# Cosformer attention ahead of a mixture of experts: the reciprocal denominators of batches 3 to 7 reach the features by DMA through DRAM

## The chip, the cores and the metric

The kernel runs on one core of a Trainium2 chip. The metric is device time in microseconds (us), lower is better; the median of six runs of the kernel before is 1002.9 us (1001.9 to 1004.23).

## The reference

Two stages follow each other. In the first, for each of 8 batches and 8 heads (576 positions s, 64 channels d), a linear attention is computed:

```python
q_p, k_p = concat([relu(x) * cos_w, relu(x) * sin_w])   # 128 features f
kv  = einsum('bhsf,bhsd->bhfd', k_p, v)
z   = k_p.sum(over s)
num = einsum('bhsf,bhfd->bhsd', q_p, kv)
den = einsum('bhsf,bhf->bhs', q_p, z) + 1e-6
attn = num / den                                        # one den for the 64 channels of a head
```

Its result, 4608 tokens x 512 channels, is the x of the second stage. There the 8 gate columns exp(x @ w_gate) are normalized over rows and columns eight times (Sinkhorn), and the output is the sum over 8 experts e of P[:, e] * (relu(x @ w1[e]) @ w2[e]), with w1[e] of 512 x 1024 and w2[e] of 1024 x 512.

## The kernel before, in words

x is held transposed in SBUF as `xT` (128 partitions hold two heads' 64 channels each; four such parts `hk` make up the 512 channels). The first phase interleaves two things in blocks j = 0 to 6, each of 16 slots: expert 0 on the token block j (512 tokens), and the attention of batch b = j + 1 (576 tokens). Slots 0 to 7 hold one `ffn1` step each (four matmuls of 512 columns, then a relu on ScalarE into `hT`); slots 8 to 15 hold half an `ffn2` each (four matmuls of 512 columns), and every second one ends with a copy of `y_ps` into the accumulator `acc`, on ScalarE for even tiles g and on VectorE for odd ones. After its matmuls a slot runs what the table `todo` lists for it, filled by `at(block, slot, fn, ...)`. Since `te`, `ve` and `se` pin the written order on TensorE, VectorE and ScalarE, the order in which these functions are called is the order of each engine's queue. POOL (GpSimd) and SP (SyncE) issue DMAs; their queues are in written order too.

The functions of the attention are, per batch:

- `load` (POOL): q, k and v of two of the four `hk`, six DMAs a batch, float32 in DRAM to float16 in SBUF, four buffers each (two batches).
- `prep_k` (relu of k, ScalarE), `prep_q` (q times cos and sin, VectorE), `prep_kv` (k times cos and sin, and v copied beside a column for z, both VectorE).
- `turn` (12 a batch): three 128-column matmuls transpose a third of a q_p into one bank of the pool `ps_s` (named small_ps, four banks), and ScalarE or VectorE, in turns, moves it with a relu to `q_pT`.
- `sums` (2 a batch): k_p times v into two banks of `ps_s`; VectorE writes `zsel`, then ScalarE `kv_sb`.
- `denominators`: 24 matmuls give den for 8 heads on 96 partitions (3 parts j of 32 rows, of which 8 differ); VectorE adds 1e-6 / 64 and takes the reciprocal, then splits it into the float16 pair `hi` and `hl`.
- `attend` (4 a batch, one for each hk): three matmuls with 0/1 weights (`spread`) bring the reciprocals of two heads to their 128 channel partitions in two banks, ScalarE copies them to `rb` in SBUF, four matmuls give the numerators in two more banks, and VectorE multiplies the two into `xT`.
- `gates`: the logits of a batch and their exp.

In block j from 1 on, `denominators` of batch j + 1 is in slot 5 and its attends are in slots 8, 10, 12 and 14, with the gates of batch j in slot 6. `ffn1` of block j + 1 reads the `xT` of batch j + 1. The last two thirds of the `turn`s of a batch, two in each of the slots 0 to 4, are in the same block as its attends; the preparation of the next batch (`ahead`) is in slots 6 to 15, its first two turns in slot 15.

After block 6 the second phase takes over the SBUF and PSUM of the first: token blocks 7 and 8 of expert 0, the Sinkhorn steps, then experts 1 to 7. `x_sums` there saves sums of `xT` to DRAM (`x_saved`) on SP's queue.

Of the kernel before, what the change touches and what calls it, by code (L numbers as in the profile page):

```python
# [25 lines left out]
def kernel(  # L26
# [10 lines left out]
    nc = tc.nc  # L37
# [44 lines left out]
    def not_before(earlier, i):  # L82

        if earlier is not None:
# [4 lines left out]
                reason="written order",  # L89
            )  # L90

    class InOrder:

        def __init__(self, engine):
# [51 lines left out]
    def ffn2(hT, w, c0, g, y_ps, fts):  # L146

        for ft in fts:
            te.matmul(
                out=y_ps,  # L150
                lhsT=hT[:, ft, c0 : c0 + P],
                rhs=w[1][:, ft, :],
                start=(ft == 0),
                stop=(ft == FT - 1),
            )
        if FT - 1 in fts:

            if g % 2 == 0:
                se.copy(out=acc(g), in_=y_ps)
            else:  # L160
                ve.tensor_copy(out=acc(g), in_=y_ps)
# [10 lines left out]
    with ExitStack() as p1:  # L172
# [4 lines left out]
        qp_pool = p1.enter_context(tc.tile_pool(name="qp_pool", bufs=3))  # L177
        qT_pool = p1.enter_context(tc.tile_pool(name="qT_pool", bufs=6))
        kv_pool = p1.enter_context(tc.tile_pool(name="kv_pool", bufs=2))
        rb_pool = p1.enter_context(tc.tile_pool(name="rb_pool", bufs=2))  # L180
        ps_y = p1.enter_context(tc.tile_pool(name="ps_y", bufs=2, space=bass.MemoryType.PSUM))
        ps_s = p1.enter_context(tc.tile_pool(name="ps_s", bufs=4, space=bass.MemoryType.PSUM))

# [1 line left out]
        loaded = {}  # L185
        sources = {"q": q, "k": k, "v": v}

        def load(b, half, names="qkv"):
            for name in names:
                x = ld.tile([P, 2, C, D], F16, name=f"{name}_ld")  # L190
                view = sources[name][b].rearrange("(hk hh) (p c) d -> (hh p) hk (c d)", hh=2, c=C)
                nc.gpsimd.dma_start(
                    out=x[:].rearrange("p hk c d -> p hk (c d)"),
                    in_=view[:, 2 * half : 2 * half + 2],
                )
                for i in range(2):
                    loaded[name, b, 2 * half + i] = x[:, i]

# [88 lines left out]
        ve.tensor_copy(out=wg[:], in_=wg_ld[:])  # L287


        kps, qps, qTs, kvs, hls = {}, {}, {}, {}, {}  # L290
        v_augs = [cs_pool.tile([P, C, D + 2], F16, name=f"v_aug{i}") for i in range(4)]
        for t in v_augs:
            ve.memset(t[:, :, D : D + 1], 1.0 / XS)

# [82 lines left out]
        def denominators(b):  # L377

            zsel = kvs[b][1]
            den_ps = ps_s.tile([P, 512], FP32, name="small_ps")  # L380
            for h in range(H):
                hk, hh = h // 2, h % 2
                for j in range(3):
                    te.matmul(
                        out=den_ps[32 * j : 32 * j + 32, 0 : C3 * HP],
                        lhsT=zsel[:, h, :],
                        rhs=qTs[b, hk][:, j * C3 : (j + 1) * C3, hh * HP : (hh + 1) * HP],
                        start=(h == 0),
                        stop=(h == H - 1),
                    )  # L390
            den = kv_pool.tile([96, C3 * HP], FP32, name="den")
            ve.tensor_scalar(
                out=den[:], in0=den_ps[0:96, 0 : C3 * HP], scalar1=1e-6 / XS, scalar2=None,
                op0=ALU.add,
            )
            ve.reciprocal(out=den[:], in_=den[:])

            hi = kv_pool.tile([96, C3 * HP], F16, name="hi")
            ve.tensor_copy(out=hi[:], in_=den[:])
            hl = kv_pool.tile([96, C3 * HP], F16, name="hl")  # L400
            ve.scalar_tensor_tensor(
                out=hl[:], in0=hi[:], scalar=lo[0:96], in1=den[:], op0=ALU.mult, op1=ALU.add
            )
            hls[b] = hl

        def attend(b, hk):

            parts = ((0, 2 * C3), (2 * C3, C))
            rb_ps = [ps_s.tile([P, 512], FP32, name="small_ps") for _ in parts]
            rb = rb_pool.tile([P, C * HP], FP32, name="rb")  # L410
            for i, (c0, c1) in enumerate(parts):
                for j in range(c0 // C3, c1 // C3):
                    te.matmul(
                        out=rb_ps[i][:, (j * C3 - c0) * HP : ((j + 1) * C3 - c0) * HP],
                        lhsT=spread[0:96, j, hk].rearrange("p hh d -> p (hh d)"),
                        rhs=hls[b][:],
                        start=True,
                        stop=True,
                    )
                se.copy(out=rb[:, c0 * HP : c1 * HP], in_=rb_ps[i][:, 0 : (c1 - c0) * HP])  # L420
            num_ps = [ps_s.tile([P, 512], FP32, name="small_ps") for _ in parts]
            for i, (c0, c1) in enumerate(parts):
                for hh in range(2):
                    te.matmul(
                        out=num_ps[i][hh * HP : (hh + 1) * HP, 0 : (c1 - c0) * HP],
                        lhsT=kvs[b][0][:, hk, hh, :],
                        rhs=qTs[b, hk][:, c0:c1, hh * HP : (hh + 1) * HP],
                        start=True,
                        stop=True,
                    )  # L430
                ve.tensor_tensor(
                    out=xT[:, hk, b * S + c0 * HP : b * S + c1 * HP],
                    in0=num_ps[i][:, 0 : (c1 - c0) * HP],
                    in1=rb[:, c0 * HP : c1 * HP],
                    op=ALU.mult,
                )
# [89 lines left out]
        for j in range(B):  # L526
            b = j + 1
            if j == 0:

                at(0, 4, lambda: begun.append(sums_begun(1, 0)))  # L530
                at(0, 5, lambda: sums_made(1, 0, begun[2]))
                at(0, 6, lambda: begun.append(sums_begun(1, 1)))
                at(0, 7, prep_q, 1, 0)
                at(0, 7, prep_q, 1, 1)
                for hk in range(HK):
                    for i in range(3):
                        at(0, 7 + hk, turn, 1, hk, i)
                    if hk == 0:
                        at(0, 7, lambda: sums_made(1, 1, begun[3]))
                    if hk < 2:  # L540
                        at(0, 7 + hk, prep_q, 1, hk + 2)
                at(0, 10, denominators, 1)
                at(0, 11, gates, 0)
                for hk in range(HK):
                    at(0, min(13 + hk, 15), attend, 1, hk)
            elif b < B:
                at(j, 0, prep_q, b, 3)
                at(j, 1, prep_kv, b, 3)
                at(j, 1, sums, b, 0)
                at(j, 3, sums, b, 1)  # L550
                for i, (hk, k_) in enumerate(turns[2:]):
                    at(j, i // 2, turn, b, hk, k_)
                at(j, 5, denominators, b)
                for hk in range(HK):
                    at(j, FT + 2 * hk, attend, b, hk)
            if j:
                at(j, 6, gates, j)
            if b + 1 < B:
                for half in range(2):
                    at(j, 2 * half if j else 3, load, b + 1, half)  # L560
                for i, (fn, hk) in enumerate(ahead):
                    at(j, NS - 10 + i if j else 11 + i // 2, fn, b + 1, hk)
                for hk, k_ in turns[:2]:
                    at(j, NS - 1, turn, b + 1, hk, k_)
        y_pss = {}
        for j in range(B - 1):
            if j:
# [172 lines left out]
    class Pair:  # L740
# [23 lines left out]
                op0=ALU.mult, op1=ALU.add,  # L764
            )

        def sums(self, after=None):
            name = "hs_last" if self.last else "hs"
            pool = u_pool if self.last else hs_pool
            S1, S2, S4 = (pool.tile([P, FH, P], F16, name=f"{name}{k_}") for k_ in (1, 2, 4))  # L770
            for out_, in0, in1, op in (
                (S1[:], self.a21, self.a22, ALU.add),
                (self.a21, self.a11, self.a21, ALU.subtract),
                (S2[:], S1[:], self.a11, ALU.subtract),
                (S4[:], self.a12, S2[:], ALU.subtract),
            ):
                i = (nc.gpsimd if self.last else ve).tensor_tensor(  # L777
                    out=out_, in0=in0, in1=in1, op=op
                )
                if self.last and after is not None:  # L780
                    tc.add_manual_dep(
                        i.ins,
                        after.ins.name,
                        mybir.DependencyInfo(
                            mybir.DependencyClass.Sync, mybir.DependencyReason.DATA
                        ),
                        reason="VectorE's sums first",
                    )
                    after = None
            self.summed = i  # L790
            self.S1, self.S2, self.S4 = S1[:], S2[:], S4[:]

# [303 lines left out]
```

The softmax here doesn't subtract the row's maximum and nothing guards it: scores larger than these inputs give would overflow.

## Time and profile before

| | |
|---|---|
| Median of six runs | 1002.9 us |
| The profiled execution's own time | 1002.74 us |
| Its span in the trace | 1001.0 us |
| TensorE busy | 983.0 us (98%) |
| VectorE, ScalarE, POOL busy | 829.4, 575.3, 60.3 us |
| Blocks 1 to 5, each | 22.2 us |
| Block 6 | 22.0 us |

PE is TensorE's matmuls, PEld its weight loads, DVE is VectorE, ACT ScalarE, SPq the DMA queue of SP. Matmuls overlap in the array, so their listed durations add up to more than the time they hold the engine; the differences between their starts are what a matmul costs its queue. A bracket at the end of a timeline line tells how long the engine sat idle before that instruction and what ended the wait. Helper objects record every engine's operations, so that nearly all instructions of the first phase have line L100; tiles (out<-in) tell them apart. TensorE's start times in one block (the one from 96.59 us, j = 3) are used below as prices.

### The profile page before, as it was taken

What the parts mean: (1) busy time and instruction counts of PE and PEld (TensorE: products, weight loads), DVE (VectorE), ACT (ScalarE), POOL (GpSimd) and SP (SyncE); (2) the same over time, 40 slices, a digit from 0 to 9 for tenths busy, and PEclk for the clock granted to TensorE, in tenths of its full rate; (3) what the DMA queues carried; (4) which work ended last, traced back from release to release, by engine and by line L of the source; (5) the groups of instructions that cost most, each with busy time, mean ns of one, the idle gap of its engine ahead of it and who ended that gap; (6) DMA issues with size and microseconds to landing.
All of it is one profiled execution on the core that took longest, in us unless ns stands there. A gap on an engine that the chain in (4) does not pass through costs nothing.

```text
span 1001.0 us, 20629 instructions
## 1 busy us (share of the span) xinstructions
PE 983.0 (98%) x8062; PEld 691.2 (69%) x8062; DVE 829.4 (83%) x1862; ACT 575.3 (57%) x1284; POOL 60.3 (6%) x82
## 2 busy tenths in 40 slices
PE   8999999999999999999999999999999999999997
PEld 7555555446777777777777777777777777777775
DVE  5888777588989887888879878888889888988887
ACT  5766666447777555555555555555555555555552
POOL 6321200001000000000000000000000000000001
PEclk8999999999999999999999999999999999999999
DMA  9956510533101331034013320043113410104535
GB/s 172 199 86 93 82 28 1 99 75 74 41 25 49 66 67 48 26 71 86 25 40 71 57 62 26 24 91 66 33 40 67 83 32 25 48 25 105 136 85 127
DMA packets 51922, 66.50 MB, mean 66 GB/s; under 512 B 4848, under 2 KB 43760, under 8 KB 51824
## 3 DMA queue, kind: packets, MB, share of 16 engines
q0 software_dynamic: 27232, 30.94, 19.9%
q1 hardware_dynamic: 24352, 33.98, 12.3%
q8 instruction: 63, 1.03, 0.4%
q14 instruction: 35, 0.29, 0.1%
q10 hardware_dynamic: 240, 0.26, 0.1%
HBM read 83.12 MB, written 12.98 MB: 96 GB/s over the span
## 4 chain that ended last, share of the span: by engine, by line
PE 72%; issue 21%; DVE 5%; ACT 1%; POOL 1%; DMA 1%; POOLq 0%; ACTq 0%; DVEq 0%
PE rows_ps L100 25%; PE h_ps L100 21%; PE copied_ps L100 8%; PE p_ps L100 8%; PE y_ps L100 5%; PE small_ps L100 5%; DVE k_p L100 1%; DMA k_ld<-in_k_dram 1%; DVE q_pT L100 1%; DVE v_aug L100 0%; DVE q_p L100 0%; DVE den L100 0%; DVE xT L100 0%; DVE acc_lo L100 0%; POOL hs_last L777 0%
## 5 line engine op out<-in xcount | busy, mean ns | idle before, releaser
L762 DVE SCALAR_TENSOR_TENSOR acc_lo<-rows_ps,P_tok,acc_lo 128x512 f32<-128x512 f32 (+1 forms) x322 | 203.1, 639 | 74.8 <-PE rows_ps L100 74.6
L100 PEld LDWEIGHTS <-H 128*128 128x128 f16 x2080 | 203.0, 98 | 83.1 <-issue 1.2
L698 ACT CAST u<-h_ps 128x384 f16<-128x384 f32 x288 | 137.8, 478 | 131.1 <-PE h_ps L100 131.1
L100 PEld LDWEIGHTS <-w1e 128*128 128x128 f16 x1632 | 155.8, 98 | 59.3 <-issue 4.9
L692 DVE CUSTOM_DVE_ANT_0 H<-p_ps,u 128x384 f16<-128x384 f32 x329 | 180.9, 550 | 6.7 <-PE p_ps L100 6.6
L100 PEld LDWEIGHTS <-hs 128*128 128x128 f16 x1500 | 146.6, 98 | 56.2
L100 PE MATMUL h_ps<-S,w1e 128*128 128x384 f16 x672 | 164.1, 326 | 1.1 <-ACT u L100 0.9
L100 PE MATMUL p_ps<-xT,T 128*128 128x384 f16 x672 | 164.1, 326 | 0.1
L100 PE MATMUL h_ps<-xT,w1e 128*128 128x384 f16 (+1 forms) x616 | 152.9, 350 | 0.0
L100 PE MATMUL rows_ps<-V,H 128*128 128x256 f16 x1000 | 150.0, 273 | 0.7 <-DVE acc_hi L762 0.7
L100 PE MATMUL rows_ps<-w2e,hs 128*128 128x256 f16 x1000 | 150.0, 273 | 0.0
L730 ACT ACTIVATE H<-h_ps 128x384 f16<-128x384 f32 x144 | 70.7, 491 | 95.1 <-PE h_ps L100 95.1
L100 PEld LDWEIGHTS <-T 128*128 128x128 f16 x1008 | 98.1, 98 | 29.3 <-issue 2.9
L100 PE MATMUL rows_ps<-w2e,H 128*128 128x256 f16 (+1 forms) x568 | 91.2, 285 | 0.0
L711 ACT COPY copied_ps<-h_ps 128x384 f32<-128x384 f32 x144 | 67.5, 468 | 35.2 <-PE h_ps L100 35.2
L721 ACT ACTIVATE H<-copied_ps 128x384 f16<-128x384 f32 x144 | 70.9, 492 | 20.3 <-PE copied_ps L100 20.3
L100 PE MATMUL h_ps<-S,T 128*128 128x384 f16 x336 | 81.8, 325 | 0.4 <-ACT copied_ps L100 0.3
L100 PE MATMUL copied_ps<-xT,w1e 128*128 128x384 f16 x336 | 82.1, 326 | 0.0
L100 PE MATMUL copied_ps<-w2e,H 128*128 128x256 f16 x504 | 75.5, 272 | 0.0
L100 PE MATMUL rows_ps<-V,hs 128*128 128x256 f16 x500 | 75.0, 272 | 0.0
L762 DVE SCALAR_TENSOR_TENSOR acc_lo<-copied_ps,P_tok,acc_lo 128x256 f32<-128x256 f32 x126 | 60.0, 476 | 0.6 <-PE copied_ps L100 0.2
L762 DVE SCALAR_TENSOR_TENSOR acc_hi<-rows_ps,P_tok,acc_hi 128x512 f32<-128x512 f32 (+1 forms) x56 | 41.3, 737 | 20.4 <-PE rows_ps L100 19.5
(126 smaller groups left out, 1020.9 us busy)
## 6 DMA issues: line engine op xcount, KB each, us to landing
S<-x_saved SPq DMA_DIRECT2D x108, 192.0 KB, 2.4
out_dram<-acc_lo SPq DMA_DIRECT2D x62, 128.0 KB, 2.4
w1e<-in_moe_w_dram POOLq DMA_DIRECT2D x7, 1024.0 KB, 8.9
w2e<-in_moe_w_dram POOLq DMA_DIRECT2D x7, 1024.0 KB, 9.4
k_ld<-in_k_dram POOLq DMA_DIRECT2D x16, 288.0 KB, 6.1
v_ld<-in_v_dram POOLq DMA_DIRECT2D x16, 288.0 KB, 6.9
q_ld<-in_q_dram POOLq DMA_DIRECT2D x16, 288.0 KB, 5.9
x_saved<-S SPq DMA_DIRECT2D x18, 192.0 KB, 1.9
```

What stands on the lines that cost most here:

```text
L100: i = getattr(self.engine, name)(*args, **kwargs)
L692: latest = ve._custom_dve(TENSOR_ADD_SAT, out=out, in0=ps[:, 0:TU], in1=t[:], s0=FP32_MAX, s1=0.0)
L698: se.copy(out=t[:], in_=ps[:, 0:TU])
L711: se.copy(out=Y[:, 0:TU], in_=X[:, 0:TU])
L721: se.activation(out=h11, in_=Y[:, 0:TU], func=AF.Relu)
L730: se.activation(out=h12, in_=X[:, 0:TU], func=AF.Relu)
L762: ve.scalar_tensor_tensor(out=a, in0=rows, scalar=P_tok[:, g, self.e : self.e + 1], in1=a, op0=ALU.mult, op1=ALU.add,)
```

## The change

For batches 3 to 7 the reciprocals no longer go through `hi`, `hl`, TensorE and ScalarE. `denominators` sends `den` (96 x 192 float32) to a DRAM tile `r` on SP's queue, and reads it back with eight DMAs, one a head, each of which writes that head's row to 64 partitions of one of four `rb` tiles. `attend` then has only its numerator matmuls and its products. For the four `rb` buffers the `v_aug` tiles move into rows of `acc_lo` that are written later.

The order changes with it. From batch 3 on the attends stand in slots 12 to 15, after everything else that needs no such wait; the denominators stand in slot 4 (in slot 5 in block 2). Batches 4 to 7 have their first eight turns and their first half of the sums in the block ahead, one turn a slot; block 2 therefore holds 18 turns, block 6 four. Of three turns two go to ScalarE, and all y copies of blocks 1 to 6 go to ScalarE. The loads of batches 4 to 7 are issued in slots 13 and 15, two blocks ahead of their attends, and each waits on the semaphore of the last VectorE instruction written before it.

```diff
+    def after(earlier, i):
+        tc.add_manual_dep(
+            i.ins, earlier.ins.name,
+            mybir.DependencyInfo(mybir.DependencyClass.Sync, mybir.DependencyReason.DATA),
+            reason="start",
+        )
...
-            if g % 2 == 0:
+            if g % 2 == 0 or TCH // P <= g < (B - 1) * TCH // P:
                 se.copy(out=acc(g), in_=y_ps)
             else:
                 ve.tensor_copy(out=acc(g), in_=y_ps)
...
-        rb_pool = p1.enter_context(tc.tile_pool(name="rb_pool", bufs=2))
+        rb_pool = p1.enter_context(tc.tile_pool(name="rb_pool", bufs=4))
...
-        def load(b, half, names="qkv"):
+        def load(b, half, names="qkv", held_back=False):
...
-                nc.gpsimd.dma_start(
+                i = nc.gpsimd.dma_start(
...
+                if held_back:
+                    after(ve.last, i)
...
-        v_augs = [cs_pool.tile([P, C, D + 2], F16, name=f"v_aug{i}") for i in range(4)]
+        lent = acc_lo[:, G_LO - 4 : G_LO, :].rearrange("p g d -> p (g d)").bitcast(F16)
+        VA = C * (D + 2)
+        v_augs = [
+            lent[:, i * VA : (i + 1) * VA].rearrange("p (c d) -> p c d", d=D + 2)
+            for i in range(4)
+        ]
...
             ve.reciprocal(out=den[:], in_=den[:])
+            if b >= 3:
+                r = dram.tile([96, C3 * HP], FP32, name="r")
+                nc.sync.dma_start(out=r[:], in_=den[:])
+                for hk in range(HK):
+                    rb = rb_pool.tile([P, C * HP], FP32, name="rb")
+                    for hh in range(2):
+                        h = 2 * hk + hh
+                        nc.sync.dma_start(
+                            out=rb[hh * HP : (hh + 1) * HP, :].rearrange(
+                                "p (j s) -> p j s", j=3
+                            ),
+                            in_=r[:].rearrange("(j r) s -> r j s", r=32)[h : h + 1].to_broadcast(
+                                [HP, 3, C3 * HP]
+                            ),
+                        )
+                    rbs[b, hk] = rb
+                return
...
             parts = ((0, 2 * C3), (2 * C3, C))
-            rb_ps = [ps_s.tile([P, 512], FP32, name="small_ps") for _ in parts]
-            rb = rb_pool.tile([P, C * HP], FP32, name="rb")
+            rb = rbs.pop((b, hk), None)
+            rb_ps = [ps_s.tile([P, 512], FP32, name="small_ps") for _ in parts if rb is None]
+            by_dma = rb is not None
+            if not by_dma:
+                rb = rb_pool.tile([P, C * HP], FP32, name="rb")
             for i, (c0, c1) in enumerate(parts):
+                if by_dma:
+                    break
...
             elif b < B:
-                at(j, 0, prep_q, b, 3)
-                at(j, 1, prep_kv, b, 3)
-                at(j, 1, sums, b, 0)
-                at(j, 3, sums, b, 1)
-                for i, (hk, k_) in enumerate(turns[2:]):
-                    at(j, i // 2, turn, b, hk, k_)
-                at(j, 5, denominators, b)
+                if j <= 2:
+                    at(j, 0, prep_q, b, 3)
+                    at(j, 1, prep_kv, b, 3)
+                    at(j, 1, sums, b, 0)
+                    at(j, 3, sums, b, 1)
+                    for i, (hk, k_) in enumerate(turns[2:]):
+                        at(j, i // 2, turn, b, hk, k_, k_ != 1)
+                else:
+                    at(j, 0, sums, b, 1)
+                    for i, (hk, k_) in enumerate(turns[8:]):
+                        at(j, i, turn, b, hk, k_, k_ != 1)
+                at(j, 5 if j <= 2 else 4, denominators, b)
                 for hk in range(HK):
-                    at(j, FT + 2 * hk, attend, b, hk)
+                    at(j, 8 + 2 * hk if j == 1 else 12 + hk, attend, b, hk)
             if j:
                 at(j, 6, gates, j)
-            if b + 1 < B:
+            if j <= 1:
                 for half in range(2):
                     at(j, 2 * half if j else 3, load, b + 1, half)
...
+            elif b + 1 < B:
+                for slot, fn, hk in (
+                    (4, prep_k, 0), (5, prep_q, 0), (6, prep_kv, 0), (6, prep_k, 1),
+                    (7, prep_q, 1), (8, prep_kv, 1), (9, prep_k, 2), (10, prep_q, 2),
+                    (11, prep_kv, 2), (11, prep_k, 3), (13, prep_kv, 3), (15, prep_q, 3),
+                ):
+                    at(j, slot, fn, b + 1, hk)
+                for i, (hk, k_) in enumerate(turns[:8]):
+                    at(j, 8 + i, turn, b + 1, hk, k_, k_ != 1)
+                at(j, 10, sums, b + 1, 0)
+            if 1 <= j and b + 2 < B:
+                for half in range(2):
+                    at(j, 13 + 2 * half, load, b + 2, half, "qkv", True)
```

In the last pair of the second phase an argument named `after` is renamed and calls the new helper; the instructions there are the same.

More of the change, by code (lines that the diff above doesn't have):

```diff
@@ L90, in not_before @@
             )
+    def after(earlier, i):
+        tc.add_manual_dep(
+            i.ins,
+            earlier.ins.name,
+            mybir.DependencyInfo(mybir.DependencyClass.Sync, mybir.DependencyReason.DATA),
+            reason="start",
+        )
     class InOrder:
@@ L287 @@
         ve.tensor_copy(out=wg[:], in_=wg_ld[:])
-        kps, qps, qTs, kvs, hls = {}, {}, {}, {}, {}
-        v_augs = [cs_pool.tile([P, C, D + 2], F16, name=f"v_aug{i}") for i in range(4)]
+        kps, qps, qTs, kvs, hls, rbs = {}, {}, {}, {}, {}, {}
+        lent = acc_lo[:, G_LO - 4 : G_LO, :].rearrange("p g d -> p (g d)").bitcast(F16)
[4 more added lines that the diff above has]
+        ]
         for t in v_augs:
@@ L765, in add, with sums @@
             )
-        def sums(self, after=None):
+        def sums(self, earlier=None):
             name = "hs_last" if self.last else "hs"
@@ L779, in sums @@
                 )
[L780 to L789, printed above, removed]
+                if self.last and earlier is not None:
+                    after(earlier, i)
+                    earlier = None
             self.summed = i
```

## The prediction

> **What bounds the kernel now.** I read the page's busy shares first, then the stretch of each token block, then one block's timeline, then its chain of waits, then the DMA view. A difference of about 0.2% (2 us) is what a measurement of this kernel can tell from no change.
>
> The page, engine totals and the DMA queues:
>
> ```profile
> PE 983.0 (98%) x8062; PEld 691.2 (69%) x8062; DVE 829.4 (83%) x1862; ACT 575.3 (57%) x1284; POOL 60.3 (6%) x82
> ...
> q0 software_dynamic: 27232, 30.94, 19.9%
> q1 hardware_dynamic: 24352, 33.98, 12.3%
> ```
>
> TensorE is busy nearly throughout; a matmul taken out of its queue is worth its place, if nothing else is late there. The change touches only the attention blocks, so the stretches (us, then busy us of PE, PEld, DVE, ACT, POOL, then granted clock, DMA share, GB/s):
>
> ```profile
> 74.40:96.59 22.19, 21.87 (x243) 11.66 (x241) 17.34 (x37) 14.35 (x33) 4.28 (x6) 1.00 0.54 82
> 96.59:118.78 22.19, 21.87 (x246) 11.67 (x244) 17.24 (x37) 14.35 (x33) 4.22 (x6) 1.00 0.55 81
> ...
> 163.20:185.20 22.00, 21.68 (x240) 11.50 (x238) 13.30 (x29) 12.03 (x29) 0.00 (x0) 1.00 0.00 1
> ```
>
> All blocks take 22.2 us at full clock, even the last, in which VectorE has 4 us less to do: TensorE sets the period, not the vector engines. The block from 96.59 us, one attend in its timeline:
>
> ```profile
> 108.76 1.03 PE L100 MATMUL y_ps<-w2e,hT 128*128 128x512 f16 x4
> ...
> 109.62 0.41 PE L100 MATMUL small_ps<-hl,acc_hi 96*128 96x192 f16 x3
> ...
> 109.96 0.44 PE L100 MATMUL small_ps<-q_pT,kv_sb 128*64 128x384 f16 x4
> 110.04 0.70 ACT L100 COPY rb<-small_ps 128x384 f32<-128x384 f32 x2 [0.49 <-PE small_ps L100]
> ...
> 110.33 1.90 PE L100 MATMUL y_ps<-w2e,hT 128*128 128x512 f16 x8
> ```
>
> Starts, not durations, give the price: the spreading matmuls hold TensorE from 109.62 to 109.96, 0.34 us; the numerators 0.37; four 512-column matmuls 0.86. In the same way from this block's other starts: a turn 0.17 (a pair, 104.45 to 104.79, 0.34), half the sums 0.68, the denominators 0.77, the gates 0.51. The pure work of a block is 16 x 0.86 + 12 x 0.17 + 2 x 0.68 + 0.77 + 0.51 + 4 x (0.34 + 0.37) = 21.28; 0.9 of 22.19 is stall. The chain of waits shows where:
>
> ```profile
> 99.30 0.47 DVE q_pT L100
> 99.77 0.67 DVE k_p L100
> 100.44 0.36 DVE v_aug L100
> 100.80 0.14 DVE zsel L100
> ...
> 100.96 0.28 ACT kv_sb L100
> ...
> 101.28 0.49 PE small_ps L100 x6
> ```
>
> VectorE brings a backlog into the block's first slots, ScalarE's kv_sb waits for its zsel, and TensorE for the PSUM bank. After that the chain is TensorE's alone.
>
> **Removed, per batch 3 to 7 (blocks 2 to 6).** Twelve spreading matmuls: 4 x 0.34 = 1.36 us of TensorE, on the path; 5 batches, **-6.8 us**. Eight rb copies of ScalarE, 4 x (0.479 + 0.324) = 3.2 us, and hi and hl of VectorE, 0.256 + 0.413 = 0.67: both beside TensorE, nothing by themselves.
>
> **Moved between engines, per block.** Two y copies go to ScalarE: VectorE -2 x 0.688, ScalarE +2 x 0.586. Turns go from 6/6 to 8 on ScalarE and 4 on VectorE: +2 x 0.500, -2 x 0.553. ScalarE ends at about 14.35 - 3.2 + 1.17 + 1.0 = 13.3 us, VectorE at 17.24 - 0.67 - 1.38 - 1.11 = 14.1, both well under 20. In block 1 the old attend stays, so ScalarE rises from 14.24 to 16.4 there, with three of its turns close together in slots 0 and 1: I price that at +0.2 us, from nothing to +0.6 (one hT eviction late).
>
> **The ledger of a new block (3 to 5).** Slot 0: 0.86 + 0.68 + 0.17; slots 1 to 3: 1.03 each; slot 4: 0.86 + 0.77, so the denominators end at 6.4 us after the block's start and the reciprocal, 0.354 + 1.349 behind that, at 8.2. Slots 5 to 7: 3.1, to 9.5. Slots 8 to 11: 4 x 1.03 + 0.68, to 14.3. Slots 12 to 15: 0.86 + 0.37 + 0.17 = 1.40, numerators done at 15.6, 17.0, 18.4, 19.8; end 19.9. Block 2 has 6 more turns and one more half of sums (21.6), block 6 has 8 and one fewer (17.9); the sum is the same.
>
> **Stalls that replace the old 0.9.** VectorE's slots 12 to 15: four xT products 4 x 0.905, k_p and v_aug 1.19, q_p 0.75, two turns 1.1: 6.7 us against TensorE's 5.6. It enters slot 12 free (its slots 8 to 11 hold 4.1 of 4.8), so it is 1 us behind at the end: the bank of attend 2 comes free 0.2 to 0.3 late in slot 15, the next block's zsel about 0.5 late, and ScalarE's kv_sb, turn and hT queue behind it. I take 0.7 a block in 3 to 5 (bounds 0.3 and 1.5), 0.9 in block 2 as now, 0.5 in block 6, which has no preparation: 3.5 against 5 x 0.9 = 4.5, **-1.0 us**. The attend in slot 15 is just ahead of ffn1, which reads hk 3 only in its fourth matmul, 0.17 + 0.64 us on; the product it needs takes 0.56: within the 0.7.
>
> **Added: the trip through DRAM.** One write of 72 KB and eight reads of 144 KB on SP's queue. Nothing else of SP's is behind them; its next work is x_saved at 186.71. The DMA view:
>
> ```profile
> S<-x_saved SPq DMA_DIRECT2D x108, 192.0 KB, 2.4
> out_dram<-acc_lo SPq DMA_DIRECT2D x62, 128.0 KB, 2.4
> ...
> x_saved<-S SPq DMA_DIRECT2D x18, 192.0 KB, 1.9
> ```
>
> The write lands 1.9 after 8.2, plus a hop: 10.2. A read every 0.55 us (the spacing of SP's stores at 902 to 911 us, 1.11 a pair, its dearest row) and 1.9 to 2.4 to land: the four rb tiles are there at about 13.4, 14.5, 15.6 and 16.7, each some 2 to 3 us ahead of its attend. The engines' own pace: 1.18 MB a batch at queue q1's 33.98 MB in 12.3% of 1001 us is 4.3 us; by its packets (192 a read, 12.3% x 16 x 1001 / 24352 = 81 ns each) 7.8 us. So a read costs 0.55 to 1.0; no row has one source row copied to 64 partitions, and I take 0.6, as the bytes and the issue agree. In block 2 the reciprocal ends at 11.8 and the tiles come 1.5 to 2 us ahead; in block 6, without turns in slots 8 to 15, attend 0 is at 14.2 and the margin about 1. The new wait stands in xT on VectorE: behind it queue a turn's eviction and k_p, and TensorE through the four small PSUM banks. If the cover goes, lateness is paid nearly one for one.
>
> The loads run on the same 16 engines: a DMA share of 0.55 in 22.2 us is 12.2 us for six, 2.0 each. Held on VectorE's slot 13 and on its last turn of slot 15, the second half goes out about 2 us into the next block and the six are done at 12 to 13 us, so write and first reads meet their end in blocks 3 to 5. The first half, out at about 18 us, has some 6 to its k in slot 4 (25.5), against landings of 6.1 and 0.72 of POOL for each issue; behind the held loads POOL has only further loads until 187.26. Two x_saved writes issued beside the expert weights at 184 to 190 us took 4.8 in the median, not 1.9; with 2.9 more on our write the first tile comes at 16.3, not 15.6, and with a slower read 1 us late: 3 us in three blocks. Packets of six loads spread over 11 us are a weaker neighbour than two 1 MB weights, so I take **+0.8 us** in all (bounds 0 and 3). The Trainium skill, DMA: Bandwidth & Descriptors, section Queues, rings and completion order, has each engine switch between queue rows in turn, a packet at a time. An estimate by that page: a read that meets a load takes 12 x (81 + 117) ns = 2.4 us (117 from q0's share over its packets), the tiles come up to 2 us later but still ahead, nothing is added, and the time would be 995.1. No row shows two queues sharing in these blocks, so my term stays between none and the 4.8 us row.
>
> Moving v_aug into acc_lo, four rb buffers and the renamed argument cost nothing: the lent rows are first written in block 7. After block 6 every step, the load of expert 1's weights included, hangs on that block's end, so the gain passes on.
>
> **Sum.** -6.8 - 1.0 + 0.2 + 0.8 = -6.8. The profiled execution took 1002.74 (span 1001.0): 995.9. The median of six, 1002.9, stands 0.16 above it: 996.0.
>
> **Rivals.**
> Slower: the broadcast reads are the bound. With a pace p per read the last tile lands at 12.1 + 8p in blocks 3 to 5 (wanted at 19.8), 15.7 + 8p in block 2 (wanted at 22.3), 12.1 + 8p in block 6 (wanted at 17.9). The lateness sums to 40p - 35.5 us; below p = 1.08 that is less than the 7.6 us won without it (6.8 + 1.0 - 0.2), above it the kernel is slower than before. At p = 1.3 it is 16.5 us, and the time 1012. For: no row with this pattern, 768-byte runs, thin margins. Against: both priced ends, 0.55 and 1.0, lie below. Chance 0.2.
> VectorE takes over: its overhang of 1.1 us a block and the late zsel are paid in full, with contention at its 3 us and block 1 at +0.4: stalls 1.5 x 3 + 0.9 + 0.9 = 6.3, so -6.8 + 1.8 + 0.4 + 3 = -1.6: 1001.1. For: slots 12 to 15 are over-full. Against: block total of 14 in 20. Chance 0.13.
> The matmuls were only filler: TensorE would have waited anyway, no gain: 1003. Against: the four attends' chain has no wait in it. Chance 0.05.
>
> **How the numbers follow.** Forecast 0.62, its own range 992 (no stall at all: -6.8 - 4.5 + 0.2 gives 991.6) to 999.6 (stalls of 1.2 in three blocks, contention 3). Left out of 992 to 1007: the far end of the slower rival, 0.13, and 0.04 below. Faster by over 0.2%: the forecast and 0.05 of the second rival, 0.67; within: 0.08 of the second and 0.04 of the third, 0.12; slower: the first rival and 0.01 of the third, 0.21.
>
> **What would show it.** Right: blocks 3 to 5 at 20.4 to 20.9 us, block 6 near 18.4, block 2 near 22.5; rb landing under 17 us into the block; xT waiting on small_ps, not on rb. Wrong: xT waiting for DMA rb by microseconds, or reads spaced at 1 us and over; kv_sb and hT waiting behind zsel for over 1 us; a changed period after 186 us.

## The result, and the profile after

The changed kernel takes 1000.71 us (median of 14 runs, 998.52 to 1002.39), the kernel before 1003.13 (32 runs, 1001.47 to 1004.23). The ratio is 0.9976, 95% interval 0.9969 to 0.9983: 2.4 us faster, a third of the 7 us forecast, and close to the bound of 0.2%.

The page's engine totals and DMA queues of the changed kernel:

```profile
PE 977.7 (98%) x8002; PEld 686.0 (69%) x8002; DVE 811.6 (81%) x1828; ACT 573.0 (57%) x1268; POOL 60.3 (6%) x82
...
q0 software_dynamic: 27232, 30.94, 19.8%
q1 hardware_dynamic: 33232, 40.25, 14.8%
```

The matmuls are gone (983.0 to 977.7 us of PE, 60 fewer), and the trip through DRAM is there (8880 more packets on q1, the queue of SP's DMAs). So the change does what it says. Its stretches, in the columns shown before (us, busy us of PE, PEld, DVE, ACT, POOL, granted clock, DMA share, GB/s), for blocks 2, 3 and 6 (the first begins 0.7 us before block 2's first ffn1, the last ends 1.5 us after block 6's end, so they are longer than the table's blocks below):

```profile
73.90:97.16 23.26, 23.26 (x291) 12.80 (x290) 17.29 (x38) 16.88 (x38) 4.77 (x7) 1.00 0.72 132
97.16:119.90 22.74, 21.00 (x235) 10.82 (x233) 14.25 (x30) 13.74 (x30) 4.24 (x7) 1.00 0.72 134
...
164.00:183.90 19.90, 19.59 (x175) 8.88 (x173) 7.88 (x18) 8.69 (x18) 0.00 (x0) 1.00 0.26 64
```

The clock is full throughout. In block 3 PE is idle for 1.7 of 22.7 us, where before it was idle for 0.3 of 22.2. From the start of one block's first ffn1 to the next block's, in each kernel's profiled execution:

| block | 1 | 2 | 3 | 4 | 5 | 6 |
|---|---|---|---|---|---|---|
| before | 22.25 | 22.19 | 22.29 | 22.19 | 22.29 | 21.86 |
| after | 21.79 | 22.53 | 22.78 | 22.45 | 21.46 | 18.58 |
| forecast | 22.4 | 22.5 | 20.4 to 20.9 | 20.4 to 20.9 | 20.4 to 20.9 | 18.4 |

Blocks 2 and 6 came as forecast, block 1 better, and blocks 3 to 5 are 4 to 5.5 us too long between them. The chain of waits of block 3 shows in what (start, duration, what):

```profile
104.63 1.36 DVE den L109
...
106.01 4.67 DMA r<-den
...
110.70 0.57 SPq L423
...
111.32 4.46 DMA rb<-r
...
115.90 0.57 DVE xT L109
...
116.52 0.59 PE small_ps L109 x5
```

The reciprocal ends 8.8 us after the block's start at 97.16; the write takes 4.67 us to land, a read 4.46, and the first product begins 18.7 us into the block, where its numerators had been forecast at 15.6. (The reciprocal itself is 0.6 later than the forecast's 8.2.) Block 6 has no loads beside it, and its chain differs in the write:

```profile
172.54 1.56 DMA r<-den
...
178.67 4.17 DMA rb<-r
```

The write lands in 1.56 us, the read still takes 4.17. (A landing is the time from a DMA's issue to its end.) Who is in flight beside block 3's write, and who waits, stands in its timeline:

```profile
96.70 0.72 POOL L201 DMA_DIRECT2D q_ld<-in_q_dram  x1 [18.28 <-DVE acc_lo L109]
...
101.21 0.72 POOL L201 DMA_DIRECT2D v_ld<-in_v_dram  x1
...
110.70 5.60 SPq L423 DMA_DIRECT2D rb<-r  x8
...
115.90 0.82 DVE L109 TENSOR_TENSOR xT<-small_ps,rb 128x384 f16<-128x384 f32 x2 [3.33 <-DMA rb<-r]
116.52 0.27 PE L109 MATMUL small_ps<-q_pT,kv_sb 128*64 128x192 f16 x2 [1.56 <-DVE xT L109]
```

The held loads go out from 96.70 on, the last at 101.21, and the write goes out at 106.01. The DMA view of 101 to 101.5 us gives that last load's landing (count, KB, us):

```profile
v_ld<-in_v_dram POOLq DMA_DIRECT2D x1, 288.0 KB, 9.7
```

So the last load lands at 110.9 us and the write, issued 4.8 us after it, at 110.7. It is the same in the other blocks: the last load lands at 87.9, 131.9 and 154.6 us in blocks 2, 4 and 5, the write at 88.1, 132.1 and 154.8. The write is done when the loads are, to within 0.3 us. SP issues eight reads in 5.6 us, 0.65 each, near the 0.6 forecast. VectorE then waits 3.33 us for the first tile, and TensorE 1.56 us for VectorE to free a small PSUM bank. From 50 to 190 us the waits sum up to (engine, what, released by: us, times, longest):

```profile
DVE xT L109 <- DMA rb<-r: 17.5, 11, 6.7
```

That is the sign named in the prediction as "wrong": xT waiting for DMA rb by microseconds. Not all of it is lateness: the longest, 6.7 us, is in block 6, where VectorE has nothing else to do; in e1 below, in which no product waits for a DMA, the same product waits 6.0 us there for its matmuls. Without that one, 10.8 us are left.

### The profile page after: what moved, and what is told of

Its sections match the earlier page's. It is cut to its first block, busy times and chain, and to the rows that moved or that the text cites. A ratio compares the mean times of both kernels' runs of the same rounds, so it can differ in the third digit from the quotient of the medians.

```text
span 999.0 us, 20494 instructions
## 1 busy us (share of the span) xinstructions
PE 977.7 (98%) x8002; PEld 686.0 (69%) x8002; DVE 811.6 (81%) x1828; ACT 573.0 (57%) x1268; POOL 60.3 (6%) x82
## 3 DMA queue, kind: packets, MB, share of 16 engines
q1 hardware_dynamic: 33232, 40.25, 14.8%
## 4 chain that ended last, share of the span: by engine, by line
issue 76%; PE 13%; DMA 4%; DVE 3%; POOL 2%; SPq 1%; ACT 1%; POOLq 0%; DVEq 0%; ACTq 0%
PE h_ps L109 5%; PE small_ps L109 4%; PE y_ps L109 2%; DMA rb<-r 2%; DMA r<-den 1%; PE rows_ps L109 1%; DVE den L109 1%; SPq L423 1%; DMA k_ld<-in_k_dram 1%; DVE xT L109 0%; POOL w2e L133 0%; PE copied_ps L109 0%; POOL w1e L127 0%; POOL acc_lo L978 0%; DVE P_tok L109 0%
## 5 line engine op out<-in xcount | busy, mean ns | idle before, releaser
L780 ACT ACTIVATE H<-copied_ps 128x384 f16<-128x384 f32 x144 | 70.8, 492 | 20.4 <-PE copied_ps L109 20.4
```

The costliest lines, as they stand in the source:

```text
L780: se.activation(out=h11, in_=Y[:, 0:TU], func=AF.Relu)
```

## The experiments

The theory after this profile (T): the tiles arrive late, and this lateness costs some 5 us. The rival (V): VectorE, over-full in slots 12 to 15, is late anyway, and the DMA only takes its place. All ratios are to runs of the kernel before on the same chip.

### Attends that wait for no DMA: e1_no_wait

```diff
+        rb_one = acc_lo[:, G_LO - 4 : G_LO, :].rearrange("p g d -> p (g d)")[:, 4 * Dm - C * HP :]
+        ve.memset(rb_one, 1.0)
...
-                    rbs[b, hk] = rb
+                    rbs[b, hk] = rb_one
```

> The write and the eight reads go out as in the changed kernel, but the attends of batches 3 to 7 multiply by a tile of ones that nothing writes later, so no product waits for a DMA (the division is left out for these batches). Theory T, the trip through DRAM is late (write 3.6 to 4.7 us, reads 4.1 to 5.7 us): blocks 3 to 5 fall from 22.8, 22.5 and 21.5 us to 20.3 to 20.8, block 6 to 18.1, and the time by 5 to 6 us below the changed kernel, to 994.5 to 996. Rival V, VectorE's slots 12 to 15 are over-full by themselves: the blocks stay over 21.5 us and the time within 1.5 us of the changed kernel.

995.5 us, ratio 0.9922 (0.9908 to 0.9935). Blocks 1 to 6 take 21.79, 22.35, 20.66, 20.56, 20.66 and 18.42 us: the forecast's blocks, with VectorE as full as in the changed kernel. V is out. The first product of block 3 begins 16.0 us into the block, for 18.7 in the changed kernel. The lateness costs 1000.7 - 995.5 = 5.2 us (5.6 if each is taken against the kernel before on its own chip), and the blocks agree: after minus this one is 0.2, 2.1, 1.9, 0.8 and 0.2 in blocks 2 to 6, together 5.2.

### Rows of 2304 bytes, and a small write: e2_rows

```diff
-                r = dram.tile([96, C3 * HP], FP32, name="r")
-                nc.sync.dma_start(out=r[:], in_=den[:])
+                r = dram.tile([H, 3, C3 * HP], FP32, name="r")
+                for j in range(3):
+                    nc.sync.dma_start(out=r[:, j], in_=den[32 * j : 32 * j + H, :])
...
-                            in_=r[:].rearrange("(j r) s -> r j s", r=32)[h : h + 1].to_broadcast(
-                                [HP, 3, C3 * HP]
+                            in_=r[h : h + 1].rearrange("r j s -> r (j s)").to_broadcast(
+                                [HP, 3 * C3 * HP]
```

The eight rows that differ are written, three writes of 6 KB for one of 72, and a read moves 64 runs of 2304 bytes instead of 192 of 768.

> r is laid out with one head's 576 reciprocals in a row (three writes of 8 x 192), so that a read has 64 runs of 2304 bytes and not 192 of 768. Theory T, with the reads' 4.2 us set by their number of runs: they land in 2.4 to 3 us, their spacing falls to 0.3 to 0.6, the third write costs 0.6 us more; tiles 1 to 2.5 us earlier, time 2 to 4 us below the changed kernel. If the landing is set by the copying of one source row to 64 partitions, it stays at 4.2 and the time within 1 us of the changed kernel. Rival V: no change either way.

996.03 us, ratio 0.993 (0.9917 to 0.9944): 4.7 us below the changed kernel, more than the 2 to 4 expected. With e9, which cannot be told from it, it is the fastest kernel here that computes the whole reference, ahead of before and of after. Blocks 3 to 5 are 20.83, 20.56 and 20.66. The waits from 50 to 190 us:

```profile
DVE xT L109 <- PE small_ps L109: 8.9, 6, 6.0
...
DVE xT L109 <- DMA rb<-r: 5.7, 5, 1.7
```

xT waits for its matmuls again (the 6.0 is the product of block 6), and for the DMA by 5.7 us instead of 10.8. Against e1 the time is 0.5 us longer, which the intervals do not tell from nothing. This trace has no landing for e2's reads and writes, so their times come from e8 and e11.

### The loads not held: e3_unheld

```diff
-                if held_back:
+                if False:
```

> The loads of batches 4 to 7 no longer wait for VectorE's last instruction, only for their buffers. Theory T: they leave in slots 6 to 15 of a block and meet the reads instead of the write; the write falls to about 2 us, the reads rise to 5 to 7; the time is between 2 us below and 4 us above the changed kernel, more likely above. Rival V: within 0.5 us of the changed kernel.

1010.75 us, ratio 1.007 (1.0057 to 1.0083), 10 us above the changed kernel where at most 4 had been expected. Without the hold POOL sends the loads as soon as their buffers are free, into the reads of blocks 2 and 3, which take 29.42 and 28.05 us; the last load is issued at 133.36, and blocks 4 to 6 take 20.92, 20.66 and 18.42, with next to no lateness. Time from issue to landing of the reads (line 423):

```profile
DMA to landing us min/median/max: 4.2/4.7/11.9
```

The writes, here 7.4 us and more behind the last load's issue (4.8 in block 3 of the changed kernel), go out after that load has landed, and all land in 1.6 us. The reads of blocks 2 and 3, with three loads among them, take 5.6 to 11.9 us. The hold is worth 9 to 10 us.

### The order without the DMA: e4_order_only

```diff
-            if b >= 3:
+            if b >= B:
```

All batches spread their reciprocals by TensorE, in the new order.

> All of the changed kernel's order, its shares of ScalarE and its held loads, but every batch spreads its reciprocals by TensorE as before; nothing goes through DRAM. Theory T: 6.8 us of TensorE come back and the lateness goes; blocks 3 to 5 at 21.7 to 22.3 us, block 6 at about 19.5; the time 1000.5 to 1002.5. Rival V: VectorE's slots 12 to 15 show all the same, and the time is 1003 or more.

1007.55 us, ratio 1.0039 (1.0026 to 1.0052), above theory T's range. The time is in rival V's, but V is out by e1, and the waits name another engine. The blocks are 21.79, 25.51, 23.28, 23.18, 23.28 and 19.42. Those waits are:

```profile
DVE xT L109 <- ACT rb L109: 25.8, 19, 5.7
...
PE small_ps L109 <- ACT rb L109: 4.7, 13, 0.5
```

ScalarE, which has its new turns and y copies, still has the eight rb copies, all in slots 12 to 15. Without the DMA, which frees ScalarE of them, this order costs 4.0 us against the kernel before. That the rb copies alone do it is read from these waits; no run tests it.

### ScalarE's share alone: e5_scalar_share

```diff
-            if g % 2 == 0:
+            if g % 2 == 0 or TCH // P <= g < (B - 1) * TCH // P:
...
-                    at(j, i // 2, turn, b, hk, k_)
+                    at(j, i // 2, turn, b, hk, k_, k_ != 1)
```

Two lines of the change on the kernel before: the y copies of blocks 1 to 6 and two of three turns go to ScalarE.

> The kernel before with two lines of the change alone: the odd y copies of blocks 1 to 6 and two turns of three on ScalarE; the spreading, the order and the loads as before. Block 1, which both kernels have with this share, went from 22.25 to 21.79 us in the changed kernel's profile. If it is the share that does it, all of blocks 1 to 6 gain 0.4 to 0.5 us and the time falls by 2 to 3 us, about as much as the whole change brought; if block 1 gained for another reason, within 0.7 us of before.

998.89 us, ratio 0.9957 (0.9945 to 0.997): 4.0 us by itself, more than the 2 to 3 expected and more than the whole change. Block 1 is 0.47 us shorter, each later block 0.64 or 0.65 (21.78, 21.55, 21.65, 21.55, 21.65, 21.21). The prediction's chain of before had begun with VectorE's backlog in a block's first slots. That wait from 74 to 185 us, in the kernel before and then in this one:

```profile
ACT kv_sb L100 <- DVE zsel L100: 9.2, 10, 1.5
```

```profile
ACT kv_sb L100 <- DVE zsel L100: 3.0, 10, 0.3
```

The stall of 0.9 us a block falls to 21.6 - 21.28 = 0.3 with a lighter VectorE. Which of the two lines brings how much was not run.

### No loads beside the trip: e6_no_loads

```diff
-            if 1 <= j and b + 2 < B:
+            if 2 <= j and b + 2 < B:
+                at(j, 13, load_again, b + 2)
+            elif 1 <= j and b + 2 < B:
```

`load_again` gives batches 5 to 7 the tiles of two batches before.

> The changed kernel without the loads of batches 5 to 7 (their attention is computed from the tiles of batches 3 and 4, loaded two batches earlier). No load is in flight when the write of blocks 3 to 5 goes out. If the loads make the trip late: write 1.6 us in blocks 3 to 6, reads about 4.3, blocks 3 to 5 at 20.5 to 21.0 us, time 995 to 997, as where nothing waits for the trip. If the reads' own 4.2 us are enough to be late: blocks 3 to 5 at 21.5 us or more, time 998 or more.

995.46 us, ratio 0.9921 (0.9908 to 0.9935), as if no attend waited. Issue to landing, 96 to 178 us (count, KB each, median us):

```profile
rb<-r SPq DMA_DIRECT2D x32, 144.0 KB, 4.2
r<-den SPq DMA_DIRECT2D x4, 72.0 KB, 1.6
```

The write lands in 1.6 us, the reads are as slow as in the changed kernel, and that is hidden (blocks 3 to 6: 20.66, 20.56, 20.66, 18.42). So either remedy is enough: no loads beside the trip, or (e2) a shorter trip.

### Which half of e2: e7_small_write and e8_long_runs

e7 has the small writes, with r's layout and the reads of the change:

```diff
-                nc.sync.dma_start(out=r[:], in_=den[:])
+                for j in range(3):
+                    nc.sync.dma_start(out=r[32 * j : 32 * j + H], in_=den[32 * j : 32 * j + H, :])
```

e8 writes all 96 rows, in three parts, and reads long runs as e2 does:

```diff
+                r = dram.tile([32, 3, C3 * HP], FP32, name="r")
+                for j in range(3):
+                    nc.sync.dma_start(out=r[:, j], in_=den[32 * j : 32 * j + 32, :])
```

> The changed kernel with only the 8 rows that differ written to DRAM, three writes of 8 x 192 in place of one of 96 x 192 (18 KB for 72); the reads as they were. If the write is late by the number of its packets behind the loads, its round trip falls from 4.7, 3.6 and 3.8 us in blocks 3 to 5 to 2.5 to 3.5 and the time by 1 to 3 us; if every write behind the loads is equally late, the two more issues cost 0.6 us and the time is 0 to 1 us above the changed kernel.

> The other half of that: all 96 rows written, in three writes of 32 x 192, into rows of 576 in DRAM, so that the reads have 64 runs of 2304 bytes. If the long runs carry the gain (996.0 with both), the time is 996 to 997.5; if the small write does, it is within 1 us of the changed kernel.

e7: 1000.87 us, ratio 0.9982 (0.9973 to 0.9991), no better than the change. Its first read goes out 3.7, 4.1 and 3.5 us after its first write in blocks 3 to 5, so a quarter of the bytes came no sooner: in each of these blocks the reads leave within 0.1 to 1.4 us after the last load has landed (109.0, 132.2 and 155.2 us). e8: 996.99, ratio 0.9942 (0.9929 to 0.9956), most of e2's gain. So the length of the reads' runs carries it. In block 4 of e8, with loads in flight:

```profile
rb<-r SPq DMA_DIRECT2D x8, 144.0 KB, 3.6
r<-den SPq DMA_DIRECT2D x3, 24.0 KB, 3.3
```

The write is still slow behind the loads; the reads take 3.6 us in the median there, where the changed kernel's took 5.2 (4.3 to 5.7).

### On top of e2: e9_rows_loads_together and e10_rows_batch2

e9 holds both halves of the loads on slot 13, so that they go out sooner; e10 sends batch 2 by DMA too, with its attends in slots 12 to 15 of block 1.

```diff
-                    at(j, 13 + 2 * half, load, b + 2, half, "qkv", True)
+                    at(j, 13, load, b + 2, half, "qkv", True)
```

```diff
-            if b >= 3:
+            if b >= 2:
...
-                    at(j, 8 + 2 * hk if j == 1 else 12 + hk, attend, b, hk)
+                    at(j, 12 + hk, attend, b, hk)
```

> Long runs and the small write together (996.0 so far), and both halves of the loads held on VectorE's slot 13, so that the second half leaves some 2 us earlier. If what lateness is left comes from the loads' tail, the write's round trip falls from 3.2 to 3.5 us towards 2.1 in blocks 3 to 5 and the time by 0.3 to 0.8 us, to 995.3 to 995.7. If the lateness that is left is the reads' own landing, as block 6 (18.9 against 18.4 us, no loads) suggests, nothing that can be told from 996.0.

> Long runs and the small write, and batch 2 goes through DRAM too, with its attends in slots 12 to 15 of block 1. TensorE loses 1.36 us in block 1 (21.8 us now). Against it VectorE's slots 12 to 15 of that block hold 3.6 us of products, 3.1 of preparation and a turn, 7.3 against TensorE's 5.0, and the tiles come about 0.4 us after the numerators. If cover is what counts: block 1 at 20.8 to 21.2, block 2 0.3 us longer, time 995.3 to 996. If VectorE decides: block 1 gains nothing, time 996 to 997.

996.01 us, ratio 0.9928 (0.9917 to 0.994), and 997.21, ratio 0.9938 (0.9927 to 0.995): neither can be told from e2's 0.993. In e9 the loads went out sooner but were not gone sooner: the last went out 2.7 us into block 3 and landed at 12.6, in e2 3.6 and 12.1, and the first read followed the first write by 4.7, 3.3 and 2.9 us in blocks 3 to 5, not by 2.1. So it does not tell what an earlier end of the loads would bring. e10's block 1 takes 21.85 us for e2's 21.78, although 1.36 us of matmuls left it: VectorE waits 4.1 us for the first tile, which comes 1.1 us after its numerators and not the 0.4 expected, and TensorE then idles 0.9 us for a product.

### What a read costs, by its form: e11_read_forms

The kernel of e6 with e1's attends, so that nothing waits for the reads and no load is beside them; each batch reads 144 KB in another form, all held on the write.

```diff
+                        if b in (5, 6):
+                            row = r[:].rearrange("(h j) s -> h (j s)", j=3)
+                            own = q[b, h].rearrange("(p c) d -> p (c d)", c=C)
...
+                        if b == 4:
+                            own = q[b, h].rearrange("(j p c) d -> p j (c d)", j=3, p=HP)
```

> No product waits for the trip (a tile of ones in its place, the division left out) and the loads of batches 5 to 7 are left out, so that the reads of four kinds can be timed by themselves, eight of 144 KB each after the same write: batches 3 and 7 one row to 64 partitions in runs of 768 bytes; batch 4 64 different rows in runs of 768; batch 5 64 different rows in runs of 2304; batch 6 one row to 64 partitions in runs of 2304. If the number of runs sets the landing: 4.0 to 4.5 us in batches 3, 4 and 7 and 2.9 to 3.4 in 5 and 6. If the copying of one row does: 2.4 in batches 4 and 5, and more in 3, 6 and 7.

One execution (996.4 us). Batches 3 to 7 in order, from the DMA view of each block:

```profile
rb<-r SPq DMA_DIRECT2D x8, 144.0 KB, 4.4
...
rb<-in_q_dram SPq DMA_DIRECT2D x8, 144.0 KB, 3.5
...
rb<-in_q_dram SPq DMA_DIRECT2D x8, 144.0 KB, 2.9
...
rb<-r SPq DMA_DIRECT2D x8, 144.0 KB, 3.2
...
rb<-r SPq DMA_DIRECT2D x8, 144.0 KB, 4.3
```

Batches 3 and 7 copy one row in runs of 768 bytes: 4.3 to 4.4. Batch 4 reads 64 rows of their own in such runs: 3.5. Batch 5, rows of their own in runs of 2304: 2.9. Batch 6 copies one row in runs of 2304: 3.2. Short runs cost 0.6 us with own rows and 1.1 with a copied one; the copying costs 0.3 us with long runs and 0.8 with short ones. Within a batch the eight reads spread (2.9 to 4.5 us in batch 4), so the 0.3 is weak. Neither expectation holds alone. The own rows are rows of the input q and the copied one is a row of r, written just before, so that their difference may belong to the source as much as to the copying; no run here separates the two.

## Why the prediction was right or wrong

**The step that failed: "Added: the trip through DRAM", the contention term.** +0.8 us was put down, with 3 as its far bound; the lateness measured 5.2 (e1 against the change). Two landings in it were too short, and together they spent each margin of 2 to 3 us about twice:
- The read's landing. 1.9 to 2.4 us came from x_saved's 192 KB; the reads took 4.2 with nothing beside them (e6). The text had said that "no row has one source row copied to 64 partitions", and bounded the pace for it but not the landing. That alone takes the cover away and no more: e6 still hides it.
- The write behind the loads. 1.9 was taken and it lands in 3.6 to 4.7 in blocks 3 to 5, against 1.6 without loads (block 6, e6). The prediction had the loads done at 12 to 13 us into a block, and about so they were (the last landed at 13.7, 11.9 and 12.2); but it had the write, out at 8.2, land at 10.2, ahead of them, and in these blocks it lands with the last of them. The 4.8 row of x_saved beside the weights, set aside as a stronger neighbour, was nearer.

Together: the first tile in block 3 at 8.8 + 4.7 + 0.6 + 4.5 = 18.6 us instead of 13.4. The writes of blocks 2 (2.27) and 6 (1.56) met the last two loads or none, and these blocks lost 0.2 each.

The Trainium skill, DMA: Bandwidth & Descriptors, section Anatomy of one DMA, fits a DMA issued by GpSimd with 2.0 us and its bytes by 436 GB/s. Carried over to SP's reads, for which it is not stated, that is an estimate of 2.3 us for 144 KB; the 2.9 of batch 5 in e11 is nearest to it, and the 4.2 of the change's reads is not what it gives. The same page, section Specifications, asks for at least 512 bytes for line rate; runs of 768 bytes meet that, and still took 0.6 to 1.1 us longer than runs of 2304. Its taking of turns by packet, which the prediction weighed as tiles up to 2 us later without harm, does not, worked out as there, give what was measured: a write that lands with the last load, and reads among loads at 5.6 to 11.9 us (e3). Why they take so long stays open.

**"Removed", -6.8, and "Stalls", -1.0.** Right where the tiles do not come late: e1's blocks 3 to 5 take 20.56 to 20.66, which is 19.92 of work and 0.7 of stall, and the sum without contention (-7.6) compares with -8.0 measured. Part of that agreement is luck, since block 1 is in it with the wrong sign.

**"Moved between engines" and +0.2 in block 1: wrong in sign.** Block 1 fell by 0.46 us, and e5 shows that the two lines are worth 4.0. The bound "from nothing to +0.6" excluded a gain for no reason: the prediction's own chain showed VectorE's backlog on the path and named kv_sb, and then priced 2.5 us of work taken off VectorE as idle time. The reading "TensorE sets the period, not the vector engines", taken from the last block, went too far: in e5 that block falls by 0.65 us like the others. It did not spoil the sum: the share takes the stall to 0.3 (e5), and with the attends packed into slots 12 to 15 it is 0.7 (e1), the size that was forecast; that the packing is what brings it back is argued, not tested. But two lines without any DMA bring half as much (4.0) as the change without lateness (8.0).

**The rivals.** The reads' pace was 0.65, so the slower rival's condition (1.08) was not met. Its form, lateness paid nearly one for one, was right in blocks 3 to 5 (the last product came 2.2, 2.0 and 1.2 us later in the block than in e1, the blocks grew 2.1, 1.9 and 0.8) and too dear in blocks 2 and 6 (0.7 later, 0.2 paid). Its formula 12.1 + 8p had the landings fixed at 1.9; they, not p, were late. V, VectorE's takeover, fell with e1. The matmuls as mere filler fell too: e1's blocks of 20.6 us are shorter than the 21.28 of work that a block of before holds.

**The range.** 1000.7 lies in it, between the forecast's own end (999.6) and the VectorE rival's 1001.1, for neither's reason.

## What to carry to other kernels

When work leaves the bounding engine for a DMA, price the whole trip (each landing with its run length and its source pattern, each queue neighbour) from rows of the same form; where no row has the form, the landing needs bounds of its own, and a margin must outlast the last load in flight: the write here was done about when that load was. Give such DMAs long runs first: here that, with the write in three parts (which alone brought nothing, e7), took back 3.7 of 5.2 us (e8). And where a chain of waits begins at the second busiest engine, try shifting its copies to the third before anything larger: two lines brought 4.0 us.

## What the runs showed of the hardware

- Reads of 144 KB on SP's queue with nothing beside them land in 2.9 to 4.4 us in the median, by their runs and their source (e11), though a read's engine time is short: q1 gained 8880 packets for 14.8% x 999.0 - 12.3% x 1001.0 = 25 us of 16 engines, 45 ns a packet (the prediction had taken 81 from the kernel before), or 0.5 us if each engine has 12 of a read's 192 packets. The rest of the landing is in no view here.
- One write of 72 KB lands in 1.6 us alone. Issued on another queue 4.8 to 8.1 us after the last of six loads, while they were still in flight, it took 2.3 to 4.7, and in blocks 2 to 5 of the changed kernel it landed within 0.3 us of the last load. Reads among loads that are not held take up to 11.9 (e3).
- Holding six loads a block on a semaphore of VectorE is worth 9 to 10 us here (e3).
